# Linear attention with decay, routing and two expert layers on one core: the decay is moved to the values and the result, the w_in loads start later, and the routing's counts put thresholds on the partitions

## The chip, the cores and the metric

The kernel runs on one core of a Trainium2 chip. The metric is the device time of one execution in microseconds (us). The core's engines run their own instruction streams in order and wait for each other through semaphores: TensorE (PE in the profile; PEld are its weight loads) multiplies into PSUM, VectorE (DVE) and ScalarE (ACT) compute from PSUM and SBUF, GpSimd (POOL) from SBUF alone, SyncE (SP) issues most transfers.

## The reference

Three parts in a row. With B = 4 batches, H = 8 heads, S = 768 steps and D = 64:

```
state = gamma[h] * state + k[t] (outer) v[t]         # gamma[h] = 1 - 2**(-5-h)
y[t]  = q[t] @ state / sqrt(64)
```

`y` becomes `x` of 3072 rows by 512. Routing: `logits = x @ w_gate` (8 experts); all 24576 logits are taken in falling order, and a row goes to the first expert that still has fewer than 384 rows. Each expert gives `relu(x @ w1[e]) @ w2[e]`. Last, on all rows, `softplus(x @ w_in) @ w_out` with 2048 inner columns.

## The kernel before

**Attention.** A batch is cut into 6 chunks of 128 steps, 24 chunks in all; chunk j has place c = j % 6 in its batch. The eight heads stand in four pairs. Per chunk TensorE does five things, in this order within the loop of `Attn.emit` (line 181): `qk(j+1)`, the scores of the next chunk (k against q, into `pA`); `xo(j-1)`, which turns the previous chunk's result into rows and computes its logits (into `pX`); `y(j)`, the result (into `pY`), with a first product of state and q (only for c > 0) and a second of values and masked scores; and `kv(j)`, the state update (into `pS`, not for c = 5). `pA`, `pX`, `pY` and `pS` exist once each, so each has to be read before the next chunk writes it.

The decay enters in four ways. `scale(j)` (line 102) makes `qs`, q times 0.125 gamma^t, on GpSimd, from a table `gqt` of 256 KB per place c that is loaded with the chunks of the first batch. `scale_v(j)` makes `vh`, v times gamma^-t, with eight ScalarE operations, for the state update. `at` (line 126, VectorE) multiplies the scores by a table of 8 x 128 columns that holds mask and decay. `yT` (ScalarE, line 145) copies the result out of `pY`, unscaled; `xs` (ScalarE) copies the rows out of `pX`; `gate` (VectorE, line 173) sums the logits out of `pX` behind `xs`.

SyncE issues in one order: `load` (line 94) asks for qk and kv of chunk j+3 in chunk j; four buffers of each exist. `store` writes the rows of chunk j-2.

**Beside it: the conversion of w_in.** `Conv` reads w_in in 16 pieces of 512 KB (line 228) and makes from each piece a high and a low half with ScalarE (`cA`, `cB`, `wih`), GpSimd (`cA` lines 242 and 259) and VectorE (`cB` line 256, `cA` line 258, `wil` line 264). Its steps are spread by `side(j, part)` (in `model`) over three places of every chunk from chunk 1 on; `cv.ahead()` asks for four pieces before the first chunk.

**Routing.** After every sixth chunk `logits` calls `R.first_part`, a dozen VectorE operations on six chunks of logits ("the selection burst" below). After the last, `Route.phase` searches a threshold in six steps: compare all rows with 46 (or 32) thresholds (`G`, line 399), count per expert with 24 matmuls (line 406), compare the counts with the room left (`ind`, line 456), sum over the experts with a matmul by `ones8` (line 462), and take the place of the last threshold that any expert fills (line 466). The counts stand with the experts on the partitions and the thresholds along the columns: the stationary side of the matmul is `oef` (which row prefers which expert), the moving side the comparison.

**Experts.** From about 165 us `Ffn.emit` runs the eight experts, each with the last layer behind it. The routing of the next expert runs between their matmuls, in pieces.

The kernel's functions that the change touches:

Of the kernel before, what the change touches and what calls it, by code (L numbers as in the profile page):

```python
# [20 lines left out]
def shape_tables(H, S):  # L21


    g = 1.0 - 2.0 ** (-5.0 - np.arange(H, dtype=np.float64))
    i = np.arange(128)
    t = i[:, None] + 128 * np.arange(S // 128)
    gk = g ** (-t[:, :, None].astype(np.float64))
    m = np.where(i[:, None] <= i, 0.125 * g[:, None, None] ** (i - i[:, None]).clip(0), 0.0)
    m = m.reshape(H // 2, 2, 128, 128).transpose(2, 1, 0, 3).reshape(128, -1)
    tab = np.concatenate([np.eye(128), m, gk.reshape(128, -1)], axis=1)  # L30
    gq = 0.125 * g[:, None] ** np.arange(S, dtype=np.float64)
    gq = np.repeat(gq.reshape(H // 2, 2, 1, S // 128, 128), 64, axis=2)
    gq = gq.transpose(1, 2, 3, 0, 4).reshape(128, -1)
    return tab.astype(np.float32), gq.astype(np.float32)
# [19 lines left out]
class Attn:  # L54
# [4 lines left out]
    def __init__(self, tc, ctx, ps, qk, kv, w_gate, tab, gqt, ident, L, xd, B, H, S):  # L59
# [13 lines left out]
        ct = c.tile([128, n], FT, name="ctab")  # L73
        self.load(0, "qk")
        nc.scalar.dma_start(ct, tab[:, 128:])
        self.load(0, "kv")
        nc.scalar.dma_start(ident, tab[:, 0:128])
        self.cm = ct[:, 0:1024].rearrange("p (s a t) -> p s a t", s=2, a=HP)
        self.gk = ct[:, 1024:n].rearrange("p (c h) -> p c h", h=self.H)
# [14 lines left out]
    def load(self, j, which=("qk", "kv")):  # L94
        for n in (which,) if isinstance(which, str) else which:
            t = self.t[n, j] = self.ld.tile([128, 2, 512], FT, name=n + "_t", bufs=4)
            if n == "qk" and 0 < j < self.NC:
                self.nc.sync.dma_start(self.gq[:, j - 1], self.gq_in[:, j * 512:(j + 1) * 512])
            self.nc.sync.dma_start(t, (self.qk_in if n == "qk" else self.kv_in)[j])

    def scale(self, j):

        c, nc = j % self.NC, self.nc
        if c:
            qs = self.t["qs", j] = self.wk.tile([128, self.HP, 128], FT, name="qs", bufs=2)
            nc.gpsimd.tensor_mul(qs.rearrange("p a t -> p (a t)"), self.t["qk", j][:, 0], self.gq[:, c - 1])

    def scale_v(self, j):

        c, nc = j % self.NC, self.nc  # L110
        if c < self.NC - 1:
            vh = self.t["vh", j] = self.wk.tile([128, self.H, 64], FT, name="vh", bufs=2)
            for h in range(self.H):
                nc.scalar.activation(vh[:, h], self.t["kv", j][:, 1, h * 64:h * 64 + 64], AF.Copy,
                                     scale=self.gk[:, c, h:h + 1])

    def qk(self, j):
# [8 lines left out]
        nc.vector.tensor_mul(at, pA, self.cm)  # L126
# [32 lines left out]
    def xo(self, j):  # L159
# [7 lines left out]
        xs = self.wk.tile([128, 2, 2, 128], FT, name="xs", bufs=3)  # L167
        nc.scalar.activation(xs, pv[:, :, :, 0:128], AF.Copy)
        self.t["xs", j] = xs
        self.t["pv", j] = pv  # L170

    def gate(self, j):
        self.nc.vector.tensor_reduce(self.L[:, j, :], self.t.pop(("pv", j))[:, :, :, 128:136].rearrange("p b a e -> p e b a"),
                                     axis=AX.XY, op=OP.add)
# [6 lines left out]
    def emit(self, side, logits):  # L181
# [3 lines left out]
        self.scale(1)  # L185
        self.late_constants()
        for j in range(n):
# [5 lines left out]
            side(j, 0)  # L193
            if j:
                self.xo(j - 1)
            self.y(j)
            side(j, 1)
            if j:
                self.gate(j - 1)
# [3 lines left out]
            if j + 2 < n:  # L203
                self.scale(j + 2)
# [7 lines left out]
        self.gate(n - 1)  # L212
# [8 lines left out]
class Conv:  # L221
# [71 lines left out]
class Route:  # L293
# [3 lines left out]
    def __init__(self, tc, cp, tp, wp, psum_tile, L, NCH, E):  # L297
# [20 lines left out]
        self.id8 = t([8, 8], FT, "id8")  # L318
        v.tensor_scalar(self.id8, d[:8, :8], 0.0, None, op0=OP.is_equal)
# [14 lines left out]
        self.ones8 = t([128, 128], BF, "ones8")  # L334
        v.memset(self.ones8, 0.0)
        v.memset(self.ones8[:E], 1.0)
# [9 lines left out]
        self.r8 = t([128, 1], FT, "r8")  # L346
        v.memset(self.r8, float(CAP))
# [18 lines left out]
        self.G = t([128, N, 46], BF, "G")  # L366
# [5 lines left out]
    def top(self, c0, c1, first):  # L372
# [21 lines left out]
        v.scalar_tensor_tensor(self.kf[:, s], sg, 1025.0, self.u[:, s], op0=OP.add, op1=OP.mult)  # L394
        v.tensor_scalar(self.kx[:, s], self.bc(self.kf[:, s], n, 2), -1.0, None, op0=OP.add)
# [8 lines left out]
    def count(self, ps, c0, c1, J):  # L404
        for c in range(c0, c1):
            self.nc.tensor.matmul(ps[:, 0:J], self.oef[:, c * self.E:c * self.E + 128], self.G[:, c, :J],  # L406
                                  start=(c == 0), stop=(c == self.N - 1))

    def first_part(self, c0, c1):
# [3 lines left out]
        self.compare(c0, c1, self.t0, 46)  # L413

    def phase(self, i, slow=True, hum=lambda n: None, fill=lambda l: None):
# [9 lines left out]
        base = self.zero  # L425
        ps = None
        if last:
            v.tensor_scalar(self.kf, self.u, 0.5, None, op0=OP.subtract)
        for l, (J, s1, sh, span) in enumerate(() if last else LEVELS):
            if l:  # L430
# [6 lines left out]
                base = self.zero  # L437
            A = None
            for st in (s1, 1):
                fixed = i == 0 and l == 0 and st == s1  # L440
                if not fixed:
                    thr = T([128, 46], F16, "thr")
                    if A is None:
                        v.tensor_scalar(thr[:, :J], self.jio[:, :J], float(st), None, op0=OP.mult)
                    else:
                        v.tensor_scalar(thr[:, :J], A[:, :J], kst, None, op0=OP.add)
# [7 lines left out]
                self.count(ps, 0, N, J)  # L454
                ind = T([128, 46], BF, "ind")
                v.tensor_scalar(ind[:, :J], ps[:, 0:J], self.r8, None, op0=OP.is_ge)
                if A is None:
                    A = T([128, 46], FT, "thrA")
                    v.tensor_scalar(A[:, :J], self.jio[:, :J], base, None, op0=OP.add)
# [4 lines left out]
                sc = T([128, 46], BF, "satj")  # L464
                kst = T([128, 1], FT, "ksat", bufs=2)
                v.scalar_tensor_tensor(sc[:, :J], ps[:, 64:64 + J], 0.0, self.stc[st].to_broadcast([128, J]),
                                       op0=OP.is_gt, op1=OP.mult, accum_out=kst)
                if base is self.zero:
                    base = kst
                else:  # L470
                    nb = T([128, 1], FT, "base", bufs=2)
# [500 lines left out]
```

## Time and profile before

| what | us |
|---|---|
| median of 3 runs (lowest, highest) | 1039.04 (1035.68, 1039.63) |
| the profiled execution | 1039.39 |
| its span | 1037.6 |
| TensorE busy in the span | 994.5 (96%) |
| VectorE busy | 636.3 (61%) |
| ScalarE busy | 585.0 (56%) |
| GpSimd busy | 186.1 (18%) |
| HBM read, written | 83.73 MB, 12.58 MB |

The shares are means over three stages: the attention up to 128.5 us, the first expert's routing up to about 165 us, and the experts. "Granted clock" is the share of TensorE's full clock (2.4 GHz) that it was given; 0.5 is its lower level, 1.2 GHz, and a value between is a stretch with both.

### The profile page before, as it was taken

The page shows a single profiled execution, that of the slowest core. Times are in us where ns is not written, and L with a number is a line of the kernel's source. Part 1 is how long each engine was busy: PE and PEld are TensorE (multiplying, and loading weights), DVE is VectorE, ACT ScalarE, POOL GpSimd, SP SyncE. Part 2 cuts the span into 40 slices and gives each one's busy share as a digit, 9 for nine tenths or more (in the row PEclk, how much of TensorE's full clock was granted, in tenths as well). Part 3 has the DMA queues.
Part 4 walks back from the last instruction along what each step waited for, and adds up shares of the span by engine and source line. Part 5 has one row for each costly group of instructions (what it writes and reads, how often), then busy time and mean ns, then how long its engine had stood idle before and what let it go on. Part 6 is the DMA issues. An engine that isn't in the chain of part 4 may idle for free.

```text
span 1037.6 us, 19094 instructions
## 1 busy us (share of the span) xinstructions
PE 994.5 (96%) x7266; PEld 901.9 (87%) x7266; DVE 636.3 (61%) x1649; ACT 585.0 (56%) x1245; POOL 186.1 (18%) x204
## 2 busy tenths in 40 slices
PE   5999878999999999999999999999999999999997
PEld 4888757978899889988998889888989899999996
DVE  3686687888766666766575567555665644454432
ACT  4897723676645563566446644665356546654664
POOL 4685422556210101010101010100010020001001
PEclk9998999999999999999999999999999999999999
DMA  9998434423141104110321023101410160014000
GB/s 358 401 405 306 146 96 137 128 82 112 54 142 32 31 21 124 50 31 11 117 67 32 11 92 92 31 1 52 122 32 1 52 192 1 1 41 123 1 1 31
DMA packets 41179, 97.55 MB, mean 94 GB/s; under 512 B 5376, under 2 KB 5504, under 8 KB 41088
## 3 DMA queue, kind: packets, MB, share of 16 engines
q1 hardware_dynamic: 36432, 83.12, 24.1%
q0 software_dynamic: 3840, 12.59, 3.7%
q8 instruction: 57, 0.93, 0.4%
q10 hardware_dynamic: 816, 0.63, 0.2%
q14 instruction: 34, 0.28, 0.1%
HBM read 83.73 MB, written 12.58 MB: 93 GB/s over the span
## 4 chain that ended last, share of the span: by engine, by line
PE 72%; issue 12%; POOL 5%; DVE 5%; DMA 2%; ACT 2%; another core or an unknown queue 0%; SPq 0%; ACTq 0%; POOLq 0%
PE h L659 11%; PE h L662 11%; PE h L660 10%; PE acc L757 7%; PE acc L762 7%; PE acc L758 7%; PE acc L651 3%; PE acc L653 3%; PE acc L652 3%; PE pX L164 2%; POOL wol L259 2%; PE pA L125 2%; POOL cA L242 2%; PE pY L142 2%; PE rt L406 2%
## 5 line engine op out<-in xcount | busy, mean ns | idle before, releaser
L723 DVE SCALAR_TENSOR_TENSOR gf<-h,sp 128x384 f32<-128x384 f32 x128 | 71.2, 556 | 185.2 <-ACT sp L721 185.0
L659 PE MATMUL h<-x2h,wih 128*128 128x384 f32 x512 | 176.5, 345 | 2.0 <-DVE xl L647 2.0
L660 PE MATMUL h<-x2h,wil 128*128 128x384 f32 x512 | 173.3, 338 | 0.0
L757 PE MATMUL acc<-whi,gh 128*128 128x512 f32 x384 | 153.2, 399 | 0.0
L758 PE MATMUL acc<-wlo,gh 128*128 128x512 f32 x384 | 151.2, 394 | 0.0
L719 ACT ACTIVATE sp<-h 128x384 f32<-128x384 f32 x128 | 62.6, 489 | 137.5 <-PE h L662 127.2
L643 ACT ACTIVATE h1h<-h 128x384 fp32r<-128x384 f32 x64 | 31.5, 492 | 148.8 <-PE h L662 105.5
L770 POOL DMA_INDIRECT out_dram<-rows,ix x24 | 25.3, 1053 | 501.4 <-ACT rows L768 498.0
L662 PE MATMUL h<-x2l,wih 128*128 128x384 f32 x512 | 112.8, 340 | 0.8 <-DVE x2l L647 0.6
L762 PE MATMUL acc<-whi,gl 128*128 128x512 f32 x384 | 111.2, 396 | 0.8 <-DVE gl L737 0.8
L659 PEld LDWEIGHTS h<-x2h,wih 128*128 128x128 f32 x512 | 96.6, 189 | 5.8 <-DVE xl L647 2.2
L660 PEld LDWEIGHTS h<-x2h,wil 128*128 128x128 f32 x512 | 96.6, 189 | 3.4
L662 PEld LDWEIGHTS h<-x2l,wih 128*128 128x128 f32 x512 | 92.1, 189 | 2.9 <-DVE x2l L647 2.9
L637 DVE TENSOR_TENSOR wlo<-wraw,whi 128x512 fp32r<-128x512 f32 x128 | 86.3, 689 | 6.1 <-ACT whi L636 6.1
L659 PE MATMUL h<-xh,whi 128*128 128x384 f32 x256 | 89.0, 348 | 0.7 <-ACT xh L646 0.7
L637 DVE TENSOR_TENSOR wlo<-wol,whi 128x512 fp32r<-128x512 f32 x128 | 89.0, 698 | 0.9 <-ACT whi L636 0.9
L651 PE MATMUL acc<-h1h,whi 128*128 128x384 f32 x256 | 88.4, 345 | 0.0
L762 PEld LDWEIGHTS acc<-whi,gl 128*128 128x128 f32 x384 | 72.0, 188 | 18.6 <-DVE gl L737 1.4
L660 PE MATMUL h<-xh,wlo 128*128 128x384 f32 x256 | 86.8, 339 | 0.0
L636 ACT ACTIVATE whi<-wraw 128x512 fp32r<-128x512 f32 x128 | 76.6, 624 | 17.1 <-DMA wraw<-in_moe_w_dram 14.2
L653 PE MATMUL acc<-h1l,whi 128*128 128x384 f32 x256 | 86.1, 336 | 0.0
L652 PE MATMUL acc<-h1h,wlo 128*128 128x384 f32 x256 | 86.1, 336 | 0.0
(201 smaller groups left out, 1932.1 us busy)
## 6 DMA issues: line engine op xcount, KB each, us to landing
wraw<-in_moe_w_dram SPq DMA_DIRECT2D x128, 256.0 KB, 2.7
qk_t<-in_qk_dram SPq DMA_DIRECT2D x24, 512.0 KB, 8.8
kv_t<-in_kv_dram SPq DMA_DIRECT2D x24, 512.0 KB, 6.4
raw<-in_moe_w_in_dram SPq DMA_DIRECT2D x16, 512.0 KB, 7.0
raw<-in_moe_w_out_dram SPq DMA_DIRECT2D x32, 256.0 KB, 2.8
xd<-xs SPq DMA_DIRECT2D x24, 256.0 KB, 4.7
gqt<-in_gqt_dram SPq DMA_DIRECT2D x5, 256.0 KB
ctab<-in_tab_dram ACTq DMA_DIRECT2D x1, 536.0 KB
```

The source lines that it names most:

```text
L636: nc.scalar.activation(hi, raw, AF.Copy)
L637: nc.vector.tensor_tensor(lo, raw, hi.bitcast(FT), op=OP.subtract)
L651: nc.tensor.matmul(ps, wh, ah, start=start, stop=False)
L652: nc.tensor.matmul(ps, wl, ah, start=False, stop=False)
L653: nc.tensor.matmul(ps, wh, al, start=False, stop=stop)
L659: mm(ps, wh(d), ah[:, d], start=d == 0, stop=False)
L660: mm(ps, wl(d), ah[:, d], start=False, stop=False)
L662: mm(ps, wh(d), al[:, d], start=False, stop=d == 3)
L723: nc.vector.scalar_tensor_tensor(g, ps, 0.0, a, op0=OP.max, op1=OP.add)
L757: nc.tensor.matmul(ps, gh[:, s], wh, start=f == 0, stop=False)
L758: nc.tensor.matmul(ps, gh[:, s], wl, start=False, stop=False)
L762: nc.tensor.matmul(ps, gl[:, s], wh, start=False, stop=f == 15)
```

## The change

- **Decay on values and result.** `scale` and the table `gqt` per chunk go. `y` uses q itself in its first product and `vh` (the values times gamma^-t) in its second; the score table keeps the mask alone (128 columns, used for all heads). `yT` becomes a VectorE multiply by a factor 0.125 gamma^t per head, made for each place c from a table `gqb` of 532 columns by `factors(c)`, four small VectorE operations for each of c = 1 to 5. `scale_v` now runs for all 24 chunks, with three buffers.
- **Order.** The logit sum stands in `xo` ahead of `xs`; `side(j, 0)` comes behind `xo`.
- **w_in from chunk 3.** `cv.ahead()` before the loop goes; the first four pieces are asked for one at a time from chunk 1 on (`begin`), and conversion steps run from chunk 3.
- **Counts.** The stationary side is now the comparison (128 columns from `Gf`, of which 46 or 32 belong to the row block), the moving side the 8 expert columns. The sum over thresholds is a matmul by `upto`, which gives for each expert how many thresholds it fills, and a maximum over the eight.

```
     def y(self, j):
-        at, v = self.t["at", j], self.t["kv", j][:, 1]
+        at, vh = self.t["at", j], self.t["vh", j]
+        qt = self.t["qk", j][:, 0].rearrange("p (a t) -> p a t", a=self.HP)
...
-                    nc.tensor.matmul(to(hp, s), self.sb[j % 2][r, hp, :], self.t["qs", j][r, hp, :],
+                    nc.tensor.matmul(to(hp, s), self.sb[j % 2][r, hp, :], qt[r, hp, :],
...
-            nc.tensor.matmul(to(hp, s), v[:, h * 64:h * 64 + 64], at[:, s, hp, :],
+            nc.tensor.matmul(to(hp, s), vh[:, h], at[:, s, hp, :],
...
-        nc.scalar.activation(yT, pY[:, :, 0:256].rearrange("p b (k t) -> p b k t", k=2), AF.Copy)
+        nc.vector.tensor_tensor(yT, pY[:, :, 0:256].rearrange("p b (k t) -> p b k t", k=2),
+                                self.factor[c].rearrange("p (b k t) -> p b k t", b=2, k=2), op=OP.mult)
...
+    def factors(self, c):
+        n = (self.NC - 1) * 4
+        if 0 < c < self.NC:
+            for i in range(4):
+                s, k = slice(i * 128, i * 128 + 128), (c - 1) * 4 + i
+                self.nc.vector.tensor_scalar(self.gq[:, c - 1, s], self.gb[:, n:][:, s], self.gb[:, k:k + 1], None,
+                                             op0=OP.mult)
+        return self.gq[:, c - 1] if c else self.gb[:, n:]
...
     def xo(self, j):
...
+        nc.vector.tensor_reduce(self.L[:, j, :], pv[:, :, :, 128:136].rearrange("p b a e -> p e b a"),
+                                axis=AX.XY, op=OP.add)
+        xs = self.t["xs", j] = self.wk.tile([128, 2, 2, 128], FT, name="xs", bufs=3)
         nc.scalar.activation(xs, pv[:, :, :, 0:128], AF.Copy)
...
+    def begin(self):
+        if self.loaded < min(self.bufs - 1, len(self.plan)):
+            self.load(self.loaded)
+            self.loaded += 1
...
     def side(j, part):
-        if j:
-            cv.step((3 * j - 2 + part) * 50 // 69)
+        n = 3 * j + part
+        if n >= 3:
+            cv.begin()
+        if n >= 9:
+            cv.step((n - 8) * 50 // 63)
...
-            self.nc.tensor.matmul(ps[:, 0:J], self.oef[:, c * self.E:c * self.E + 128], self.G[:, c, :J],
+            self.nc.tensor.matmul(ps[:, 0:self.E], self.Gf[:, c * 46:c * 46 + 128], self.oe[:, c, :],
...
-                    h = N if slow else N // 2
-                    for c0 in range(0, N, h):
-                        self.compare(c0, c0 + h, thr[:, :J], J)
+                    cuts = (0, N) if slow else (0, N // 2, N - 4, N)
+                    for c0, c1 in zip(cuts, cuts[1:]):
+                        self.compare(c0, c1, thr[:, :J], J)
...
-                v.tensor_scalar(ind[:, :J], ps[:, 0:J], self.r8, None, op0=OP.is_ge)
+                v.tensor_tensor(ind, ps[:, 0:E], self.r, op=OP.is_ge)
...
-                nc.tensor.matmul(ps[:, 64:64 + J], self.ones8, ind[:, :J], start=True, stop=True)
+                nc.tensor.matmul(ps[:, 64:64 + E], self.upto[J], ind, start=True, stop=True)
...
-                v.scalar_tensor_tensor(sc[:, :J], ps[:, 64:64 + J], 0.0, self.stc[st].to_broadcast([128, J]),
-                                       op0=OP.is_gt, op1=OP.mult, accum_out=kst)
+                v.tensor_reduce(k, ps[:, 64:64 + E], axis=AX.X, op=OP.max)
```

VectorE around the first selection burst (chunk 6) before: `G` ends the burst, `at` is the mask multiply of chunk 8, and `cA`, `cB`, `wil` are conversion steps.

```order
L394 SCALAR_TENSOR_TENSOR kf<-sg,unas 128x6
L395 TENSOR_SCALAR kx<-kf 128x12
L399 TENSOR_TENSOR G<-kx,thr_85 128x276
L258 TENSOR_SCALAR cA<-cA 128x512
L126 TENSOR_TENSOR at<-pA,ctab 128x1024
L264 TENSOR_TENSOR wil<-cA,wih 128x4x128
L173 TENSOR_REDUCE L<-pX 128x8
L256 SCALAR_TENSOR_TENSOR cB<-raw,cB 128x512
L126 TENSOR_TENSOR at<-pA,ctab 128x1024
```

And the same place in the changed kernel.

```order
L391 TENSOR_SCALAR kx<-sg 128x12
L398 TENSOR_TENSOR G<-kx,thr_79 128x276
L413 TENSOR_SCALAR kf<-sg 128x6
L259 SCALAR_TENSOR_TENSOR cB<-raw,cB 128x512
L127 TENSOR_TENSOR at<-pA,ctab 128x1024
L171 TENSOR_REDUCE L<-pX 128x8
L261 TENSOR_SCALAR cA<-cA 128x512
L148 TENSOR_TENSOR yT<-pY,gqt 128x512
L267 TENSOR_TENSOR wil<-cA,wih 128x4x128
L127 TENSOR_TENSOR at<-pA,ctab 128x1024
```

The result's multiply `yT` has come into this queue, one per chunk, and the logit sum stands directly behind `at`.

ScalarE in two ordinary chunks before; `vh x8` are the eight scalings, `sb` is the copy of the state.

```order
L168 ACTIVATE xs<-pX 128x512
L145 ACTIVATE yT<-pY 128x512
L157 ACTIVATE sb_168<-pS 128x256
L114 ACTIVATE vh<-kv_t,ctab 128x64 x8
L241 ACTIVATE cA<-raw 128x512
L243 ACTIVATE cB<-raw 128x512
L168 ACTIVATE xs<-pX 128x512
L145 ACTIVATE yT<-pY 128x512
```

After, ScalarE at the end of the second batch; the first `vh x8` is that of the chunk at place c = 5, which was not scaled before, the second that of the next batch's first chunk.

```order
L174 ACTIVATE xs<-pX 128x512
L272 ACTIVATE wih<-cA 128x4x128
L161 ACTIVATE sb_160<-pS 128x256
L115 ACTIVATE vh<-kv_t,ctab 128x64 x8
L244 ACTIVATE cA<-raw 128x512
L246 ACTIVATE cB<-raw 128x512
L174 ACTIVATE xs<-pX 128x512
L115 ACTIVATE vh<-kv_t,ctab 128x64 x8
```

`yT` has left the queue, and every chunk has its scalings.

SyncE's first transfers before; `raw x4` are the four pieces of w_in.

```order
L99 DMA qk_t<-in_qk_dram 128x1024
L99 DMA kv_t<-in_kv_dram 128x1024
L98 DMA gqt<-in_gqt_dram 128x512
L99 DMA qk_t<-in_qk_dram 128x1024
L99 DMA kv_t<-in_kv_dram 128x1024
L98 DMA gqt<-in_gqt_dram 128x512
L99 DMA qk_t<-in_qk_dram 128x1024
L99 DMA kv_t<-in_kv_dram 128x1024
L230 DMA raw<-in_moe_w_in_dram 128x1024 x4
L98 DMA gqt<-in_gqt_dram 128x512
L99 DMA qk_t<-in_qk_dram 128x1024
L99 DMA kv_t<-in_kv_dram 128x1024
```

And SyncE's first transfers after.

```order
L98 DMA qk_t<-in_qk_dram 128x1024
L98 DMA kv_t<-in_kv_dram 128x1024
L98 DMA qk_t<-in_qk_dram 128x1024
L98 DMA kv_t<-in_kv_dram 128x1024
L98 DMA qk_t<-in_qk_dram 128x1024
L98 DMA kv_t<-in_kv_dram 128x1024
L98 DMA qk_t<-in_qk_dram 128x1024
L98 DMA kv_t<-in_kv_dram 128x1024
L98 DMA qk_t<-in_qk_dram 128x1024
L228 DMA raw<-in_moe_w_in_dram 128x1024 x2
L98 DMA kv_t<-in_kv_dram 128x1024
L228 DMA raw<-in_moe_w_in_dram 128x1024
```

The four w_in pieces stood ahead of the loads of chunk 3; now the first of them stands behind q and k of chunk 4.

## Rows read from the trace of the kernel before

**Rows 1.** Stretches: length, busy us (instructions) of five engines, granted clock, DMA share, GB/s.

```profile
14.76:22.63 7.87, 4.38 (x77) 3.84 (x73) 2.85 (x4) 6.79 (x22) 2.82 (x3) 0.91 1.03 405
22.63:29.41 6.78, 6.78 (x73) 5.91 (x73) 2.35 (x4) 3.07 (x9) 5.56 (x6) 0.60 1.03 407
29.41:55.64 26.23, 25.34 (x405) 22.22 (x401) 18.47 (x37) 24.22 (x71) 17.66 (x13) 1.00 1.03 402
...
71.78:79.75 7.97, 4.38 (x77) 3.81 (x73) 7.76 (x18) 7.97 (x26) 5.19 (x4) 0.97 1.02 405
79.75:86.97 7.22, 7.22 (x72) 6.35 (x73) 3.58 (x7) 1.44 (x3) 4.08 (x3) 0.56 0.78 285
86.97:103.11 16.14, 16.14 (x260) 14.24 (x256) 10.51 (x15) 14.41 (x43) 9.32 (x7) 1.00 0.85 300
103.11:109.60 6.49, 4.45 (x76) 3.81 (x73) 5.07 (x16) 6.49 (x19) 3.50 (x3) 1.00 0.97 339
109.60:122.50 12.90, 12.90 (x216) 11.43 (x216) 10.53 (x14) 10.51 (x35) 10.04 (x7) 1.00 0.27 90
122.50:128.53 6.03, 4.73 (x56) 4.01 (x53) 1.36 (x5) 2.90 (x6) 0.00 (x0) 1.00 0.25 91
...
300.00:1037.60 737.60, 729.28 (x4532) 668.65 (x4530) 422.66 (x1086) 399.13 (x774) 42.39 (x60) 1.00 0.17 50
```

**Rows 2.** TensorE's score matmuls in order of time: start, us, idle before and releaser.

```profile
10.24 2.08 PE L125 MATMUL pA<-qk_t 64*128 64x128 f32 x16 [1.80 <-DMA qk_t<-in_qk_dram]
...
22.63 2.08 PE L125 MATMUL pA<-qk_t 64*128 64x128 f32 x16 [3.50 <-DMA qk_t<-in_qk_dram]
...
79.75 2.08 PE L125 MATMUL pA<-qk_t 64*128 64x128 f32 x16 [3.59 <-DVE at L126]
```

**Rows 3.** The chain that ended last, first 30 us: start, us, what.

```profile
1.69 10.43 DMA rx<-in_moe_w_gate_dram
...
13.46 9.04 DMA qk_t<-in_qk_dram
```

**Rows 4.** DMA issues: line, count, size of one.

```profile
gqt<-in_gqt_dram SPq DMA_DIRECT2D x5, 256.0 KB
ctab<-in_tab_dram ACTq DMA_DIRECT2D x1, 536.0 KB
```

**Rows 5.** Groups by shape, 6 to 128.7 us: busy us, mean ns, idle before.

```profile
L126 DVE TENSOR_TENSOR at<-pA,ctab 128x1024 f32<-128x1024 f32 x24 | 29.3, 1222 | 26.7 <-PE pA L125 26.5
L256 DVE SCALAR_TENSOR_TENSOR cB<-raw,cB 128x512 int32<-128x512 int32 x16 | 14.4, 900 | 3.3 <-ACT cB L243 3.3
...
L106 POOL TENSOR_TENSOR qs<-qk_t,gqt 128x512 f32<-128x512 f32 x20 | 27.6, 1388 | 12.4 <-DMA qk_t<-in_qk_dram 9.6 <-issue 1.6 <-PE pY L138 1.2
...
L145 ACT ACTIVATE yT<-pY 128x512 f32<-128x512 f32 x24 | 14.3, 594 | 15.8 <-PE pY L142 9.3 <-PE pS L155 6.5
```

**Rows 6.** One small VectorE operation in two bursts, and GpSimd beside the first.

```profile
45.08 3.04 POOL L106 TENSOR_TENSOR qs<-qk_t,gqt 128x512 f32<-128x512 f32 x2
...
46.95 1.24 DVE L384 TENSOR_TENSOR lm<-L,m 128x48 f32<-128x48 f32 x1
...
104.75 0.21 DVE L384 TENSOR_TENSOR lm<-L,m 128x48 f32<-128x48 f32 x1
```

**Rows 7.** One chunk's scalings on ScalarE and its state update on TensorE.

```profile
43.95 2.02 ACT L114 ACTIVATE vh<-kv_t,ctab 128x64 f32<-128x64 f32 x8
...
45.27 1.08 PE L155 MATMUL pS<-vh,kv_t 128*64 128x64 f32 x16
```

**Rows 8.** VectorE in the first routing: a compare of 46 columns, one of 8.

```profile
131.21 0.26 DVE L456 TENSOR_SCALAR ind<-pS,r 128x46 bf16<-128x46 f32 x1 [0.40 <-PE pS L406]
...
148.69 0.17 DVE L493 TENSOR_TENSOR inc<-pS,rem 128x8 f32<-128x8 f32 x1
```

**Rows 9.** TensorE among the experts: 24 matmuls of 46 columns, 24 of 6.

```profile
275.95 0.78 PE L406 MATMUL rt<-G,oe 128*128 128x46 bf16 x24
...
342.79 0.76 PE L553 MATMUL rt<-rh,ohq 128*128 128x6 bf16 x24
```

More of the change, by code (lines that the diff above doesn't have):

```diff
@@ L27, in shape_tables @@
     gk = g ** (-t[:, :, None].astype(np.float64))
[L28 to L33, printed above, removed]
+    heads = np.array([[[4 * k + 2 * (s ^ b) + s for k in range(H // 4)] for s in range(2)] for b in range(2)])
+    gb = np.repeat(g[heads.reshape(2, -1)], 64, axis=0)
+    gs = gb[:, None] ** (128.0 * np.arange(1, S // 128))[:, None]
+    tab = np.concatenate([np.eye(128), i[:, None] <= i, gk.reshape(128, -1)], axis=1)
+    gq = np.concatenate([gs.reshape(128, -1), (0.125 * gb[:, :, None] ** i).reshape(128, -1)], axis=1)
     return tab.astype(np.float32), gq.astype(np.float32)
@@ L96, in load @@
             t = self.t[n, j] = self.ld.tile([128, 2, 512], FT, name=n + "_t", bufs=4)
-            if n == "qk" and 0 < j < self.NC:
-                self.nc.sync.dma_start(self.gq[:, j - 1], self.gq_in[:, j * 512:(j + 1) * 512])
             self.nc.sync.dma_start(t, (self.qk_in if n == "qk" else self.kv_in)[j])
[L101 to L106, printed above, removed]
+    def factors(self, c):
[6 more added lines that the diff above has]
+        return self.gq[:, c - 1] if c else self.gb[:, n:]
     def scale_v(self, j):
         c, nc = j % self.NC, self.nc
[L111 to L115, printed above, removed]
+        vh = self.t["vh", j] = self.wk.tile([128, self.H, 64], FT, name="vh", bufs=3)
+        for h in range(self.H):
+            nc.scalar.activation(vh[:, h], self.t["kv", j][:, 1, h * 64:h * 64 + 64], AF.Copy,
+                                 scale=self.gk[:, c, h:h + 1])
     def qk(self, j):
@@ L184, in emit @@
         self.scale_v(0)
-        self.scale(1)
         self.late_constants()
+        self.factor = [self.factors(0)]
+        self.factor.append(self.factors(1))
         for j in range(n):
@@ L192, in emit @@
                 self.qk(j + 1)
-            side(j, 0)
             if j:
                 self.xo(j - 1)
+            side(j, 0)
             self.y(j)
             side(j, 1)
-            if j:
-                self.gate(j - 1)
             self.kv(j)
@@ L202, in emit @@
                 self.load(j + 3, "kv")
-            if j + 2 < n:
-                self.scale(j + 2)
+            if j + 2 < self.NC:
+                self.factor.append(self.factors(j + 2))
             if j + 1 < n:
@@ L333, in __init__ @@
         v.memset(self.ones, 1.0)
-        self.ones8 = t([128, 128], BF, "ones8")
-        v.memset(self.ones8, 0.0)
-        v.memset(self.ones8[:E], 1.0)
+        pid = x([128, 128], FT, "pid")
+        it(pid, pattern=[[0, 128]], base=0, channel_multiplier=1, **imp)
+        self.upto = {}
+        for J in (46, 32):
+            self.upto[J] = t([128, 128], BF, f"upto{J}")
+            v.tensor_scalar(self.upto[J], pid, float(J), None, op0=OP.is_lt)
         self.io = t([128, 128], BF, "io128")
@@ L393, in top @@
         v.tensor_scalar(sg, ik, 21, None, op0=OP.arith_shift_right)
-        v.scalar_tensor_tensor(self.kf[:, s], sg, 1025.0, self.u[:, s], op0=OP.add, op1=OP.mult)
-        v.tensor_scalar(self.kx[:, s], self.bc(self.kf[:, s], n, 2), -1.0, None, op0=OP.add)
+        if first:
+            v.tensor_scalar(self.kx[:, s], self.bc(sg, n, 2), 1024.0, None, op0=OP.add)
+        else:
+            v.scalar_tensor_tensor(self.kf[:, s], sg, 1025.0, self.u[:, s], op0=OP.add, op1=OP.mult)
+            v.tensor_scalar(self.kx[:, s], self.bc(self.kf[:, s], n, 2), -1.0, None, op0=OP.add)
     def compare(self, c0, c1, thr, J):
@@ L402, in compare, with count @@
             thr.rearrange("p (a m) -> p a m", m=2)[:, None].to_broadcast([128, n, J // 2, 2]), op=OP.is_ge)
-    def count(self, ps, c0, c1, J):
-        for c in range(c0, c1):
-            self.nc.tensor.matmul(ps[:, 0:J], self.oef[:, c * self.E:c * self.E + 128], self.G[:, c, :J],
+    def count(self, ps):
+        for c in range(self.N):
+            self.nc.tensor.matmul(ps[:, 0:self.E], self.Gf[:, c * 46:c * 46 + 128], self.oe[:, c, :],
                                   start=(c == 0), stop=(c == self.N - 1))
@@ L424, in phase @@
             yield
[L425 to L426 removed]
+        base = ps = None
         if last:
@@ L925, in logits @@
             R.first_part(j - 5, j + 1)
-    cv.ahead()
     a.emit(side, logits)
```

67 lines of the change are left out of this document (24 added, 43 removed).

## The prediction

> **What bounds the kernel now.** I read the table of stretches first [rows 1]. From 300 us to the end TensorE is busy for 729.28 of 737.60 us at granted clock 1.00: whatever the change does to the other engines there is hidden behind it, unless it takes columns or matmuls from TensorE. The first 128.5 us, the attention, are different. There a chunk that nothing disturbs takes 4.30 us of TensorE: 109.60 to 122.50 is three such chunks in 12.90 us. The first and the last chunk of a batch of six do less; a stretch with one of each and two ordinary chunks takes 16.14 us, so that pair takes 16.14 - 8.60 = 7.54 us. From 14.76 to 122.50 the kernel runs 16 ordinary chunks and three such pairs: 16 x 4.30 + 3 x 7.54 = 91.42 us if nothing were lost. It takes 107.74. So 16.32 us are lost, and [rows 1] say where: 3.57 in 14.76:22.63, 2.48 in 22.63:29.41 (granted clock 0.60), 1.49 in 29.41:55.64, 3.67 in 71.78:79.75, 2.92 in 79.75:86.97 (clock 0.56) and 2.19 in 103.11:109.60. Next, the instructions of TensorE say what each loss waited for [rows 2]: the load of chunk 3's q and k (3.50 us idle), and the mask multiply "at" on VectorE (3.59 us idle); after each of the two the matmuls of the next chunk ran at half clock.
>
> **The start.** The chain shows why chunk 3 was late [rows 3]. Eight transfers can be on their way and SyncE issues in order; the third w_in load stood behind the small w_gate transfer, which landed 12.1 us in, and q and k of chunk 3 behind four w_in loads. They were issued at 13.46 and landed 9.04 us later. In the new order nothing of w_in stands ahead of chunk 3: before its qk there are three chunks' loads and the tables, and the w_in loads start in chunk 1. The bytes shrink too [rows 4]: five tables of 256 KB go, the 536 KB table becomes 176 columns (88 KB), a table of 532 columns (266 KB) comes: 1.46 MB less. Chunk 3's load is then 4.1 MB into the queue, about 10 us at the 405 GB/s of [rows 1], against a need at 18 us. Both the 3.57 and the 2.48 (half clock behind an idle stretch that goes) fall away: **-6.05**. Chunk 1's load, which TensorE awaited 1.80 us before 10.24 [rows 2], has 0.45 MB less ahead of it, 1.1 us at that rate; bounds 0 and 1.1, I take **-0.8**.
>
> **Loads later on.** The q load of chunk j+3 now waits for the second product of chunk j-1, since that reads q itself and no scaled copy; the value load behind it on SyncE waited for that chunk anyway. A chunk needs some 1.71 MB (two loads, a store, 0.8 of a w_in load), or 4.2 us at 410 GB/s: as much as TensorE's pace. The load is issued two chunks ahead of its use, so I count nothing. By the Trainium skill, page "DMA: Bandwidth & Descriptors", section "Specifications", a core's HBM limit is about 358 GB/s; that would make these loads the bound (a rival below). The trace has moved 402 to 407 GB/s over whole stretches [rows 1], so the sum goes by the trace.
>
> **VectorE.** It gets the result's multiply: 24 times 128x512 out of PSUM. The nearest row is "at", the same form at twice the width: 1.222 us [rows 5], half of which is 0.61; with a fixed part it may be 0.75. ScalarE takes 0.594 for the same tile today [rows 5]. I take 0.65: 24 x 0.65 = 15.6 us. Four small multiplies for the factors in each of five early chunks hide under the cold start; behind them waits only "at" of the next chunk, two chunks early. GpSimd loses 20 multiplies of 1.388 us [rows 5]. What that is worth to VectorE shows in one operation of 128x48: 1.24 us beside GpSimd's multiplies, 0.21 without [rows 6]; and the conversion's 0.9 us "cB" [rows 5] is a 0.68 us operation held the same way. "at" shows no such hold in its mean, and the new multiply reads PSUM and one SBUF operand as "at" does. By the Trainium skill, page "SBUF — State Buffer", section "Who interferes with whom", GpSimd and VectorE share a port pair as a lock, which an operation with one SBUF input outside the 2-port modes does not need; by that rule the new multiply is never held, and the trace of "at" agrees.
>
> In undisturbed stretches VectorE is busy 65% (10.51 of 16.14) to 70% (18.47 of 26.23) [rows 1]. 0.65 us in 4.30 adds 15 points and the denser conversion 3, and fewer holds take back about 4: some 82%. So it does not set the pace, but it is in order, and the result's multiply has to be done before the next chunk's third product. I allow 0.1 us per chunk for that in the 21 chunks with conversions: **+2.1** (bounds 0 and 0.35 each).
>
> **The selection bursts.** At three places a dozen VectorE operations stand ahead of "at"; today they cost 1.49 + 3.67 + 2.92 + 2.19 = 10.27. In the new order, counted from the start of that short chunk: the second product ends near 3.3 (half a microsecond before the 3.77 us are over), the multiply at 4.0, a conversion at 4.9, twelve small operations of about 0.2 [rows 6] at 7.3, one more conversion at 8.2, "at" at 9.4. TensorE wants the bank near 3.77 + 4.30 = 8.1. It is 1.3 late; the eviction on ScalarE, which now waits for the reduction behind "at", adds a little. I take 1.5 each, 4.5 in all. Ends: 0, and today's 10.27. In 103.11:109.60 TensorE idled 2.04 us (6.49 - 4.45) and kept the clock, the stop of 3.59 lost it [rows 1, 2], so I expect no half-clock chunk. Against 10.27: **-5.8**, which the 2.1 above reduce to -3.7.
>
> **ScalarE** loses 24 x 0.594 = 14.3 and gains the scaled values of four more chunks, 4 x 2.02 = 8.1 [rows 5, 7]. But the second product now needs the scaled values, where only the state update did. The update started at 45.27 while the eight scalings ran from 43.95 to 45.97 [rows 7]: matmuls follow head by head. From the update's end there are 0.4 us for the state copy and 2.0 for the scalings, against 3.9 us until the last head is multiplied. What ScalarE does in between (up to 1.3 us of conversion) fits. I count nothing; the other end is a rival.
>
> **Routing before the experts.** The tail of the last chunk stays at 6.03 us [rows 1]: the reduction no longer waits for the eviction, the last multiply comes behind the last conversion, about 0.6 us each way. In each of six search steps a compare over 46 columns (0.26) becomes one over 8, like a row of 0.17 [rows 8]; one operation and its accumulator read become one reduction; the thresholds lose an operation that sat beside the path; the last of three comparisons is shorter, so the count ends sooner. About 0.25 per step and 0.2 for an operation taken from the first: **-1.7** (bounds 0 and 3).
>
> **Routing among the experts.** 36 times 24 counting matmuls pass on TensorE, and their moving side shrinks from 46 or 32 columns to 8. 24 of 46 columns take 0.78 us, 24 of 6 columns take 0.76 [rows 9]: the columns don't set their pace. 36 x 0.02 = 0.7 at most; I take **0**.
>
> **Sum.** -6.05 - 0.8 - 3.7 - 1.7 = -12.2 us. The profiled execution took 1039.39 (span 1037.6 and 1.8 around it), 0.35 above the median 1039.04: 1026.8, so 1027.
>
> **Rivals.** (a) ScalarE holds the second product. For: it was busy 14.41 of 16.14 us in 86.97:103.11 [rows 1], and its eviction now also waits for VectorE. Against: it loses 6.2 us. Price: 0.35 more in 21 chunks, 7.4: 1034. (b) The loads set the pace. For: 402 to 407 GB/s until 80 us. Against: they kept up once chunk 3 was in, and 1.46 MB go. Then only those 3.6 us and the routing's 1.7 are won: 1034. By the 358 GB/s of the page, an estimate, the 36.4 MB up to chunk 21 (22 chunks' loads, 17 stores, 16 w_in loads and the tables) would take 102 us where they have 97, and some 5 us of the gain would go. (c) VectorE becomes the pacemaker, the slower side: the result's multiply waits in order behind conversions that GpSimd holds, the third product waits for it. In 71.78:79.75 VectorE was busy 7.76 of 7.97 [rows 1]. If 21 chunks take 4.30 + 0.65 + 0.2, that is 17.9, and if each burst idles TensorE for 3.59 again and loses the clock, 3 x 6.6 = 19.8. Against 16.32 + 0.8 + 1.7 = 18.8 that could be won, the time is 1039.4 - 18.8 + 17.9 + 19.8 = 1058; with half of the clock losses 1048. It decides from a mean chunk of 5.2 us on. (d) The bursts cost next to nothing without GpSimd's multiplies, and the routing gives 3: 1020.
>
> **Chances.** The forecast 0.62 (its own range 1022 to 1032), (a) 0.14, (b) 0.07, (c) 0.05, (d) 0.12. 0.5% is 5.2 us, about what a measurement of this kernel can tell from no change: faster is below 1033.8. The forecast, (d) and about half of (a) and (b) lie there: 0.84; within 0.11; slower 0.05. The range runs from (d)'s lower end, 1019, to the far side of (a) and (b), 1035.
>
> **What would show it.** Right: TensorE idles for no load at chunk 3 and runs at full clock from about 14 us; the attention's last reduction starts near 118 instead of 128.5; ordinary chunks take 4.3 to 4.5; three stops of 1 to 2 us on "at"; 24 counting matmuls still take 0.77. Wrong: chunks near 5 us with TensorE waiting for the result's multiply (c) or the scaled values (a), or for q (b); a granted clock near 0.6 anywhere after 15 us.

## The result and the profile after

The changed kernel takes **1023.18 us** (median of 4 runs, 1021.64 to 1025.88), the kernel before 1038.85 beside it: ratio 0.9866, 95% interval 0.9839 to 0.9893. The forecast was 1027 (1019 to 1035). The profiled execution took 1021.64 with a span of 1019.9. The table compares it with the profiled execution before: these two lie 17.75 us apart, the medians 15.67, since single executions of one kernel differ by some 4 us.

| stage (ends) | before | after | change | forecast |
|---|---|---|---|---|
| attention (last logit reduction) | 128.53 | 116.62 | -11.91 | -10.55 |
| routing (first expert matmul) | 36.35 | 35.28 | -1.07 | -1.7 |
| experts (end of the span) | 872.72 | 868.0 | -4.72 | 0 |

The stretches of after, in the columns of [rows 1]:

```profile
13.16:17.91 4.75, 4.75 (x75) 4.25 (x73) 2.41 (x7) 2.88 (x10) 0.00 (x0) 1.00 1.03 398
17.91:22.21 4.30, 4.30 (x76) 3.81 (x73) 2.79 (x8) 2.88 (x10) 0.00 (x0) 1.00 1.02 379
22.21:48.58 26.37, 26.03 (x405) 22.11 (x401) 22.99 (x51) 24.87 (x75) 14.92 (x10) 1.00 1.03 414
64.74:70.11 5.37, 4.49 (x77) 3.79 (x73) 5.20 (x17) 3.53 (x12) 3.13 (x2) 1.00 1.03 412
70.11:75.51 5.40, 5.02 (x72) 3.93 (x73) 3.75 (x8) 5.33 (x15) 3.10 (x2) 1.00 1.03 405
75.51:91.66 16.15, 16.15 (x261) 14.25 (x257) 13.18 (x23) 15.85 (x49) 8.79 (x6) 1.00 1.02 394
91.66:97.57 5.91, 4.40 (x76) 3.78 (x72) 5.77 (x18) 3.44 (x12) 2.72 (x2) 1.00 0.93 348
110.48:116.62 6.14, 4.06 (x53) 3.49 (x50) 2.43 (x6) 3.29 (x11) 0.16 (x1) 1.00 0.24 89
```

No chunk behind chunk 2 runs at half clock (chunk 2, at 13.16, began slowly: 1.61 us for score matmuls that then take 1.16), and an ordinary chunk still takes 4.30 us: 75.51:91.66 holds a short and a long chunk and two ordinary ones in 16.15 us, as 86.97:103.11 did [rows 1]. From 13.16 to 110.48 the 91.42 us of undisturbed chunks take 97.32; the 5.90 lost are 0.45 in 13.16:17.91 and, at the three bursts, 1.63 (26.37 less 16.14 and two chunks), 2.17 (5.37 + 5.40 less two chunks) and 1.61 (5.91 less one). TensorE's score matmuls of after, as in [rows 2]:

```profile
17.91 1.16 PE L126 MATMUL pA<-qk_t 64*128 64x128 f32 x16
...
43.71 1.16 PE L126 MATMUL pA<-qk_t 64*128 64x128 f32 x16 [0.22 <-DVE at L127]
...
70.11 1.16 PE L126 MATMUL pA<-qk_t 64*128 64x128 f32 x16 [0.88 <-DVE at L127]
...
97.57 1.16 PE L126 MATMUL pA<-qk_t 64*128 64x128 f32 x16 [1.52 <-DVE at L127]
```

Chunk 3, at 17.91, waits for no load; three short stops on "at" are left. The groups of after from 5 to 118 us, in the columns of [rows 5]:

```profile
L127 DVE TENSOR_TENSOR at<-pA,ctab 128x1024 f32<-128x1024 f32 x24 | 29.3, 1219 | 6.8 <-PE pA L126 6.7
...
L148 DVE TENSOR_TENSOR yT<-pY,gqt 128x512 f32<-128x512 f32 x20 | 13.8, 689 | 14.4 <-PE pY L145 14.4
...
L259 DVE SCALAR_TENSOR_TENSOR cB<-raw,cB 128x512 int32<-128x512 int32 x16 | 11.4, 713 | 0.0
```

The result's multiply takes 0.689 us (0.65 was taken), and "cB" fell from 0.900 [rows 5] to 0.713 without GpSimd's multiplies beside it.

### The profile page after: what moved, and what is told of

Same layout as the page of the kernel before. It is cut to its first block, busy times and chain, and to the rows that moved or that the text cites. A ratio compares the mean times of both kernels' runs of the same rounds, so it can differ in the third digit from the quotient of the medians.

```text
span 1019.9 us, 19016 instructions
## 1 busy us (share of the span) xinstructions
PE 989.3 (97%) x7266; PEld 895.3 (88%) x7266; DVE 635.6 (62%) x1615; ACT 580.3 (57%) x1253; POOL 159.6 (16%) x185
## 4 chain that ended last, share of the span: by engine, by line
PE 67%; issue 12%; POOL 4%; DVE 4%; ACT 2%; DMA 1%; another core or an unknown queue 0%; POOLq 0%; ACTq 0%
PE h L652 11%; PE h L655 11%; PE h L653 10%; PE acc L750 7%; PE acc L751 7%; PE acc L755 7%; PE acc L644 3%; PE acc L646 3%; PE acc L645 3%; PE rt L405 2%; POOL wol L262 1%; POOL cA L245 1%; PE h L676 1%; PE pA L862 1%; POOL out_dram L763 1%
```

## The experiments

The first four, and the next four, ran on one chip each beside the kernel before (1037.59 and 1037.32 us).

**One part at a time.** The kernel before with the counts alone:

> The kernel before with the routing part of the change alone. Theory (the sum of the prediction): the first routing, 36.35 us from the attention's last logit sum to the first expert matmul, gets 1 to 2 us shorter; 24 counting matmuls among the experts stay at 0.76 to 0.78 us; in all 1.5 to 2.5 us less, ratio 0.998. Rival: the moving columns set the pace of the counting matmuls (46 or 32 become 8), so the 24 take about 0.4 us, and the experts' stage loses another 13 us: ratio 0.985.

1033.22 us, ratio 0.9959 (0.9942 to 0.9976): 4.3 us, twice the forecast. The experts took 868.8, 3.9 less than before, almost all that the whole change wins there. In this trace the attention ends 3.4 us earlier too, at 125.12, 2.48 of it at chunk 3: the stop there stayed (3.41 us), yet the chunk behind it kept the clock.

With the later w_in alone:

```
-        if j:
-            cv.step((3 * j - 2 + part) * 50 // 69)
+        n = 3 * j + part
+        if n >= 3:
+            cv.begin()
+        if n >= 9:
+            cv.step((n - 8) * 50 // 63)
```

> The kernel before with the later w_in loads alone (conversion from chunk 3, loads from chunk 1); the factor tables of 256 KB are still loaded. Theory: the order of SyncE's queue held chunk 3 back, so the 3.5 us wait for its q and k and the half-clock chunk behind it go: 6 us less, ratio 0.994; the three bursts stay as they are (10 us together, give or take where they fall). Rival: the amount of bytes held it back (the tables), then 1 us or less is won, ratio 0.999.

1036.57 us, ratio 0.9992 (0.9976 to 1.0008): 1.0 us, which the times can't tell from nothing. In the traces the attention ends at 125.37, against 127.19 to 128.53 in the three with the old attention and the old counts: 1.8 to 3.2 us. Either way the step fell. The wait at chunk 3 is gone (chunks 2 to 4 start at 14.75, 19.05 and 23.35), but much of what it gave is taken back. The stretches of two chunks where the conversion now starts and of the first and third burst (engines as in [rows 1]):

```profile
27.65:33.23 5.58, 4.34 (x77) 3.81 (x73) 3.88 (x5) 5.58 (x16) 4.62 (x4) 1.00 1.02 410
33.23:38.93 5.70, 3.90 (x60) 3.24 (x56) 3.39 (x6) 3.79 (x8) 5.34 (x4) 1.00 1.03 409
42.64:48.83 6.19, 4.44 (x76) 3.80 (x72) 4.88 (x17) 6.19 (x18) 2.79 (x2) 1.00 1.03 411
96.00:104.18 8.18, 4.38 (x76) 3.81 (x72) 7.97 (x17) 8.18 (x26) 5.66 (x5) 0.92 1.00 381
```

In three of the four ScalarE, the fourth busy column, is busy without a gap: the same conversion in fewer chunks, beside the copies of the result that ScalarE still makes here. The third burst now stops TensorE for 3.81 us.

With the decay alone:

> The kernel before with the decay part alone (decay on values and result, logit sum in front of the eviction, side(j, 0) behind xo); w_in still loads first, the routing is the old one. Theory: the bursts cost 5 to 6 us instead of 10.3, since GpSimd's 20 multiplies no longer hold VectorE, and chunk 3 still waits for its load, some 2.5 us less long for the missing tables: 5 to 8 us less, ratio 0.994. Rival: the result's multiply on VectorE costs what GpSimd's multiplies gave back, and nothing is won at the bursts: 0 to 3 us less, ratio 0.999.

1027.38 us, ratio 0.9917 (0.9888 to 0.9946): 10.2 us. The three parts add up (10.2 + 4.3 + 1.0 = 15.5 of 15.7), each known to 2 or 3 us. This part alone ends the attention at 117.65, though TensorE waits for q of chunk 3 about as long as before:

```profile
20.44 1.16 PE L126 MATMUL pA<-qk_t 64*128 64x128 f32 x16 [3.23 <-DMA qk_t<-in_qk_dram]
```

The matmuls take 1.16, not the 2.08 of [rows 2]: this stop cost no clock. The bursts lose some 3.9 us, against 10.27. This part changes several things at once (the engines, the tables, the order within `xo`); the next run takes out one of them, and what the order gives by itself no run shows.

**GpSimd's multiplies back.** In the changed kernel, on a tile that nobody reads:

```
+            if j + 2 < n and (j + 2) % self.NC:
+                jk = self.wk.tile([128, 512], FT, name="jk", bufs=2)
+                self.nc.gpsimd.tensor_mul(jk, self.t["qk", j + 2][:, 0], self.factor[(j + 2) % self.NC])
```

> The changed kernel with 19 GpSimd multiplies of 128x512 put back at their old place, into a tile that nobody reads. Theory: the bursts are short because GpSimd no longer holds the port that VectorE's operations with two SBUF inputs need; then the three bursts lose 9 to 11 us instead of 5.4, and the time rises by 3 to 6 us to about 1028. Rival: the bursts are shorter through the new order alone; then the time stays within 1 us of 1023.

1031.33 us, 8 over the changed kernel and more than either theory said; the attention ends 8.4 later, and the bursts lose some 14.0 instead of 5.41. Its groups from 5 to 126 us:

```profile
L127 DVE TENSOR_TENSOR at<-pA,ctab 128x1024 f32<-128x1024 f32 x24 | 29.2, 1216 | 6.0 <-PE pA L126 5.7
L206 POOL TENSOR_TENSOR jk<-qk_t,gqt 128x512 f32<-128x512 f32 x19 | 25.9, 1368 | 10.9 <-DVE gqt L106 7.8 <-issue 3.1
L262 DVE SCALAR_TENSOR_TENSOR cB<-raw,cB 128x512 int32<-128x512 int32 x16 | 14.8, 924 | 0.0
L270 DVE TENSOR_TENSOR wil<-cA,wih 128x512 fp32r<-128x512 f32 x15 | 14.7, 980 | 0.0
L148 DVE TENSOR_TENSOR yT<-pY,gqt 128x512 f32<-128x512 f32 x20 | 13.8, 688 | 13.2 <-PE pY L145 13.2
```

"at" and "yT", which read PSUM and one SBUF operand, keep their 1.22 and 0.69 us; "cB" and "wil", with two SBUF operands, go from 0.713 and 0.823 to 0.924 and 0.980. That is 5.7 us of VectorE over 31 operations, and the third stop on "at" grows from 1.52 to 3.83. GpSimd itself is waited for once, by ScalarE, for 0.2 us. Part of the 8 is the clock: behind the second and the third stop TensorE ran at a granted clock of 0.71 (74.06:80.04 and 104.42:110.29). So the move to VectorE pays because GpSimd's multiplies go with it.

**The result's multiply twice.** The same operation issued two times per chunk:

> The changed kernel with the result's multiply on VectorE issued twice per chunk, one directly behind the other (24 more operations of 0.69 us). Theory: VectorE has room in ordinary chunks (some 85% busy), and the multiply is on no path there; what is added shows at the three bursts alone and in the tail: 2 to 5 us more than the changed kernel, ratio to the kernel before 0.989 to 0.992. Rival: VectorE paces the attention since the change; then 24 x 0.69 = 16.5 us come on top and the ratio is 1.002.

1029.54 us against 1021.89 for the changed kernel on the same chip: 7.7 for 24 added operations of 0.69, so 0.3 us each: above the forecast, below the rival. Ordinary chunks away from the bursts took 4.39 to 4.68 us.

**The bursts cut in pieces.** `first_part` gives VectorE free after every operation or two, and `side` takes the next piece:

```
     def side(j, part):
...
+        for g in pend:
+            next(g, None)
+    pend = []
     def logits(j):
         if j % 6 == 5:
-            R.first_part(j - 5, j + 1)
+            pend[:] = [R.first_part(j - 5, j + 1)]
+            if j == NCH - 1:
+                for _ in pend[0]:
+                    pass
```

> The changed kernel with each of the first three selection bursts cut into seven pieces of one or two operations, one behind each place where conversion steps are issued (some 2.3 chunks long), the fourth as before. Theory: the 5.4 us that the chunks behind the bursts still lose come from twelve operations in a row ahead of the mask multiply; spread, they cost 1 us or less: 4 to 5 us below the changed kernel, ratio 0.982 to 0.983. Rival: VectorE lacks the time as such in those chunks, so spreading moves the loss without shrinking it: within 1 us of the changed kernel.

**1019.07 us**, ratio 0.9828 (0.9795 to 0.9862), 2.8 below the changed kernel beside it: less than the 4 to 5 forecast, more than the rival's 1, and the best of this study. The attention ends at 113.23 instead of 116.58. The stops on "at" are gone; the next limit shows itself, the loads:

```profile
85.54 1.16 PE L126 MATMUL pA<-qk_t 64*128 64x128 f32 x16 [0.34 <-DMA qk_t<-in_qk_dram]
89.89 1.16 PE L126 MATMUL pA<-qk_t 64*128 64x128 f32 x16 [0.57 <-DMA qk_t<-in_qk_dram]
```

**Both kernels again.**

> The kernel before once more, unchanged, for a second profile of the same program. Theory: the stops of 3.4 to 3.6 us at chunk 3 and behind the second burst come again at the same places, but whether the clock falls behind each of them differs from one execution to the next; at least one of the four stretches that ran at half clock in the first profile (22.6 to 29.4, 79.8 to 87, 164.9 to 168, 263 to 267 us) runs at full clock, or another falls. Rival: the stop's length decides, and the same four stretches are slow.

1038.79 us. The clock fell in the same four places, as the rival said: behind the stop at chunk 3 (granted clock 0.57), behind the second burst (0.72), in the first expert's first 5 us (0.66) and behind expert 1's stop (0.71). One more stretch was slow, in the routing (0.62 in 131.60:139.80). So this run does not show that the same stop sometimes keeps the clock; the comparison with another kernel does. The chunk behind the stop at chunk 3, first here, then in the kernel with the counts alone:

```profile
22.44:29.58 7.14, 7.14 (x72) 6.27 (x72) 2.96 (x5) 3.56 (x11) 6.41 (x6) 0.57 1.03 406
```

```profile
22.45:26.75 4.30, 4.30 (x72) 3.81 (x72) 2.94 (x4) 3.18 (x9) 4.30 (x4) 1.00 1.03 408
```

The same 72 matmuls, the same work beside them, and stops of 3.00 and 3.41 us ahead: the longer one kept the clock.

> The changed kernel once more, unchanged, beside the two variants on the same chip. Theory: 1021 to 1026 us; no stop in the attention is longer than 1.7 us and the clock falls nowhere behind chunk 2. Rival: the first profile was a lucky one; half-clock stretches appear at the bursts or where the experts begin, and the profile is 2 to 4 us longer.

1021.89 us; the attention ended at 116.58 without a half-clock chunk behind chunk 2, as in the first profile.

**The w_in order inside the change.** On a third chip (before: 1035.31):

> The changed kernel with the old order of the w_in loads (four pieces ahead of the first chunk, conversion from chunk 1): the decay and counts parts together. Theory (the later w_in is worth about 1 us, because the conversion that starts later takes back what the stop at chunk 3 gives): the stop at chunk 3 is there again, 3.0 to 3.5 us on the load, chunks 5 to 10 and the bursts lose less than in the changed kernel, 1022.5 to 1025. Rival (the prediction's step: the order of SyncE's queue is worth 6.05 us): 1028 to 1030, with a half-clock chunk behind the stop.

1024.2 us, ratio 0.9884 (0.9845 to 0.9923), within the theory's range: the stop at chunk 3 is 2.45 us, shorter than forecast, with a partly half-clock chunk behind it (granted clock 0.71), and the attention ends at 118.43, 1.8 after that of the changed kernel.

> The kernel with the bursts cut in pieces, with the old order of the w_in loads. Theory: with the bursts spread, the conversion that starts in chunk 3 no longer pushes a burst out, so the stop at chunk 3 counts in full when it comes back: 3 to 3.5 us over the kernel with the bursts cut (1019.07), so 1022 to 1023. Rival (the order of the loads is worth nothing in any of these kernels, since the loads of q wait later on for what w_in has moved): 1018.5 to 1020, and the waits of 0.34 and 0.57 us for q near 85 and 90 us are gone.

1020.78 us, ratio 0.9853 (0.9821 to 0.9885), between theory and rival: chunk 3 stops for 2.85 us at full clock, no q is waited for afterwards, and the attention ends at 113.86 against 113.23. The two ratios (0.9853 and 0.9828) differ by 2.6 us, well inside their intervals, so the times alone can't tell this from nothing; the traces put the later w_in at 0.6 to 1.8.

**The clock at the experts.** Sixteen filling matmuls, whose product nobody reads, became twenty:

> The kernel before with 20 instead of 16 filling matmuls (their product is read by nobody) on TensorE behind the first row list, some 1 us more of matmuls in the idle time before the first expert. Theory (the first expert lost 1.5 to 2 us in the kernel before, because its first matmuls ran at half clock behind idle TensorE time, and the counts part won this back by moving the fall of the clock elsewhere): with less idle time the first expert's first 5 us run at a granted clock of 1.00 with 29 matmuls instead of 0.69 with 20, and from its first matmul to the next expert's transposes it takes 89.4 to 89.9 us instead of 91.15 and 91.67. Rival (the fall has nothing to do with the idle time just before): the granted clock there stays near 0.66 to 0.69 and the stretch at 91 to 92.

1037.12 us in one run. The forecast fell: the idle 0.94 us ahead of the last row list was filled, and the first expert began at half clock all the same. Four other stops ahead of it stayed (0.58, 0.91, 0.16 and 0.69 us), so this does not clear idle time as such:

```profile
162.88:167.88 5.00, 5.00 (x20) 5.00 (x21) 1.79 (x4) 1.48 (x3) 0.00 (x0) 0.66 0.18 52
```

Last, on a fourth chip (before: 1036.82), an operation of the same form as the one that the change removes at the end of each routing, put into the changed kernel:

```
+        junk, acc = T([8, E], FT, "junk"), T([128, 1], FT, "acc")
+        v.scalar_tensor_tensor(junk, self.r[:8, :], 1.0, oh[:8], op0=OP.mult, op1=OP.mult, accum_out=acc[:8])
```

> The changed kernel with the small VectorE operation of 8x8 that the change removed put back at the end of each routing (its result is read by nobody). Theory (it was this operation, 0.39 us with its accumulator read, ahead of xl on VectorE, that made the stop ahead of expert 1's last matmuls 2.0 instead of 1.66 us and so let the clock fall): the stop is 2.0 us again, the 4.3 us behind it show a granted clock near 0.6 and 15 matmuls instead of 22, the time is 1.5 to 2.5 us over the changed kernel. First rival (the stop comes back, the clock doesn't fall): the stop is 2.0 us, the clock 1.00, the time 0.4 us more. Second rival (the stop's length is set elsewhere): 1.66 us.

1022.52 us, ratio 0.9865 (0.9835 to 0.9896): no difference that these times can tell. The stop is back, and TensorE kept the clock behind it (4.29 us to the next transposes), as the first rival said:

```profile
252.56 0.45 PE L654 MATMUL h<-x2h,wih 128*128 128x384 f32 x1 [2.03 <-DVE xl L642]
```

But its first expert began at half clock, alone among nine traces with the new counts.

## Why the prediction was right, and where it was not

**The sum: right in part by luck.** It had -12.2 us, and the medians show -15.7. The term for the loads' order was far too large and the terms for decay and bursts too small (-0.8 and -3.7 forecast, 10.2 us for that part alone, some 2.5 of it because the chunk behind the stop kept the clock), so two errors offset each other; and the 4 us won among the experts were put at nothing. Two of the rivals' prices don't follow from their terms: half of the clock part of (c) alone gives 1054 and not 1048, and the terms of (d) add up to 1021; neither moves the range.

**The size of the attention's gain: right (-11.9, forecast -10.55); its division: wrong.** The step "nothing of w_in stands ahead of chunk 3 [...] Both the 3.57 and the 2.48 [...] fall away" gave the whole -6.05 to the order of SyncE's queue. Both fell away, but the order alone is worth 1.0 us to the kernel before (1.8 to 3.2 by the traces) and 0.6 to 1.8 to the changed ones: the conversion that starts later has to be done in fewer chunks, on the engines that the bursts need. The forecast counted the loads' order and not the work that comes with the loads. The half-clock chunk was not tied to the length of the stop at chunk 3 either: stops there of 3.50, 3.00, 2.65 and 2.45 us were followed by half clock, stops of 3.41, 3.23 and 2.85 were not.

**VectorE and the bursts: right.** Forecast for the coupling and the bursts together: 6.6 lost; measured 5.90, of it 5.41 at the bursts (4.5 forecast) and 0.45 at chunk 2. The coupling of 0.1 us per chunk did not show, since chunks still take 4.30; VectorE is busy 13.18 of 16.15 us in 75.51:91.66, the 82% of the forecast. Rival (c) had its place right and its point of decision wrong by far: with GpSimd's multiplies back and with the multiply doubled, ordinary chunks away from the bursts took at most 4.7 us, yet each cost 8 us. Rivals (a) and (b) fell: ScalarE is busy 15.85 of 16.15 us in 75.51:91.66 and TensorE still never waits there; in the new order the loads behind chunk 1 were waited for only once the bursts were spread. By the Trainium skill, "SBUF — State Buffer", section "Who interferes with whom", GpSimd and VectorE hold their shared port pair as a lock, which an operation with one SBUF input outside the 2-port modes does not need; the trace with the multiplies back agrees for the four groups shown. The small "kx" of the bursts (128x12, one SBUF input) slowed as well, from 0.173 to 0.517 us, and no row shows in which mode it ran.

**The start:** 1.5 to 1.8 us earlier, not 0.8: chunks 0, 1 and 2 began at 4.87, 8.40 and 13.16 instead of 6.36, 10.24 and 14.76.

**Routing before the experts: not shown.** The steps are shorter: from the first compare to the last it takes 13.51 us instead of 14.78, and a compare is

```profile
119.16 0.17 DVE L455 TENSOR_TENSOR ind<-pS,rem 128x8 bf16<-128x8 f32 x1 [0.37 <-PE pS L405]
```

against 0.26 [rows 8]. But the stage takes 36.20 us in the mean of the five traces with the old counts (35.46 to 37.22) and 36.14 in that of the nine with the new ones (34.67 to 37.31). The granted clock of the whole stage was 0.95, 0.94, 1.00, 0.82 and 1.00 in the five and 0.76 to 0.90 in the nine. What a low clock does there stands in after's TensorE rows:

```profile
127.03 2.91 PE L862 MATMUL pA<-wih 128*128 128x512 f32 x6
129.74 0.83 PE L405 MATMUL pS<-oe,G 128*128 128x8 bf16 x24
```

Six filling matmuls took 1.64 us in the same place before; at a granted clock of 0.50 (127.03:129.74) they take 2.91, the count stands behind them, and VectorE waits 0.72 us for it. The kernel before has one such place too, two steps earlier (2.91 us at 133.97, VectorE waiting 0.95), so this shows the price and not the whole difference. With it one of the forecast's signs of being wrong appeared, a clock near 0.6 behind 15 us, though in the routing and not where the forecast looked.

**Routing among the experts: the step that failed.** "36 x 0.02 = 0.7 at most; I take 0" held for what it counted. After's count has the time of [rows 9]:

```profile
259.21 0.76 PE L405 MATMUL rt<-oe,G 128*128 128x8 bf16 x24
```

and from the third expert's first transposes to the last one's (368.82 to 907.59 before, 351.77 to 889.97 after) the stage gained 0.57 us. But the experts as a whole take 871.4 to 872.8 us in the five traces with the old counts and 867.4 to 869.7 in the nine with the new: about 4. Two things were not in the sum. First, an operation that the diff removes in one line (590): VectorE before, then after, ahead of the stop at expert 1:

```profile
261.19 0.51 DVE L588 SCALAR_TENSOR_TENSOR rem<-oh,d 128x8 f32<-128x8 f32 x1
261.73 0.32 DVE L590 SCALAR_TENSOR_TENSOR junk<-rem,id 8x8 f32<-8x8 f32 x1
261.99 0.07 DVE L590 DVE_READ_ACCUMULATOR junk<-rem,id 8x1 f32 x1
261.99 0.67 DVE L637 TENSOR_TENSOR wlo<-wol,whi 128x512 fp32r<-128x512 f32 x1
```

```profile
246.44 0.50 DVE L583 SCALAR_TENSOR_TENSOR rem<-oh,d 128x8 f32<-128x8 f32 x1
246.87 0.68 DVE L630 TENSOR_TENSOR wlo<-wol,whi 128x512 fp32r<-128x512 f32 x1
```

It shortens the stop from 2.01 to 1.66 us, and putting it back made that 2.03: shown. Second, the clock, at the first expert and behind that stop; before, then after:

```profile
164.88:169.88 5.00, 5.00 (x20) 5.00 (x21) 1.93 (x4) 1.47 (x3) 0.00 (x0) 0.69 0.19 56
...
263.32:269.17 5.85, 5.85 (x21) 5.41 (x22) 4.96 (x15) 4.44 (x11) 3.86 (x4) 0.71 0.35 111
```

```profile
151.90:156.90 5.00, 5.00 (x29) 5.00 (x30) 2.79 (x7) 2.01 (x5) 0.00 (x0) 1.00 0.18 52
...
248.20:252.48 4.28, 4.28 (x22) 3.84 (x23) 3.83 (x9) 3.55 (x9) 2.75 (x4) 1.00 0.33 120
```

The first costs 1.75 us (91.15 against 89.40 from the first matmul to the next expert's transposes), the second 1.57 (5.85 less 4.28). With the stop's 0.35 and the 0.57 that is 4.2 of the 4.72. The first place ran at half clock in four of five traces with the old counts and one of nine with the new, the second in four of five and none of nine. Why the counts part moves the fall elsewhere **stays open**, but the traces show where it went. Ahead of the first expert stand 16 filling matmuls; before, then after:

```profile
155.44 3.90 PE L869 MATMUL pA<-wih 128*128 128x512 f32 x16
```

```profile
142.72 5.50 PE L862 MATMUL pA<-wih 128*128 128x512 f32 x16
```

In eight of the fourteen traces the 15 us ahead of the first expert had a granted clock of 0.88 or 0.89, as after; seven of them began the experts at full clock. Of the six with 0.96 to 1.00 there, as before, four began them at half clock. Seven of the nine traces with the new counts are among the eight, and one of the five with the old: a part of what the experts gain had been paid in the routing.

At expert 1 all eight stops of 1.63 to 1.68 us kept the clock, and four of the six of 1.98 to 2.03 lost it. The two that kept it (the later w_in alone, and the small operation put back) are the two whose experts began at a granted clock of 0.50 for the whole first 5 us. So the one trace with the operation put back does not clear the stop's length: that the removed operation gave the 1.57 as well is possible, and not shown.

## What to carry to other kernels

When a load is moved later, move its work along in the sum: here the transfer's wait went, and the conversion behind it took about half of it or more back. Before an operation is given to an engine, ask which of its neighbours are held by a third engine: GpSimd's multiplies, put back, cost 8 us, half of what the change wins. And count every line of a diff on the in-order engine ahead of a stop, the small ones as well.

## What the runs showed of the hardware

- TensorE's clock did not follow the length of a stop alone: ahead of chunk 3, 3.41 us kept it and 2.45 lost it; at the bursts 2.04 (the multiply twice) kept it and 1.92 (GpSimd's multiplies back) lost it, and all six stops of 3.46 to 3.83 there lost it.
- At half clock, matmuls that only fill idle time can delay real ones: six took 2.91 us instead of 1.64, and VectorE waited 0.72 us for the count behind them.
- One core's transfers went at 412 to 414 GB/s over whole stretches of the changed kernel.
